# The tails' product of the second layer moved ahead of the seven products, with the first sum of weights brought behind it

## The chip, the cores and the metric

The kernel runs on one core of one Trainium2 chip. The metric is device time in microseconds for one execution of the whole program, all eight batches. The engines' names are those of the profile: PE is TensorE (matmuls; PEld its weight loads), DVE is VectorE, ACT is ScalarE, POOL is GpSimd, and SP is SyncE, which here issues the DMAs (its queue is shown as SPq).

## The reference

The inputs q, k and v have 8 batches, 8 heads, 576 tokens and 64 dimensions a head, in float32. Attention keeps for each query the 32 largest scores:

```python
scores = scale * np.matmul(q, k.transpose(0, 1, 3, 2))
kth = np.partition(scores, -top_k, axis=-1)[..., -top_k:-top_k + 1]
scores = np.where(scores >= kth, scores, -1000000000.0)
# softmax over the last axis, then
attn_out = np.matmul(attn, v)
```

Its result, with the heads side by side, is x: 576 tokens of 512 numbers for each batch. Then follow a Fourier mix and a two-layer perceptron:

```python
X = np.fft.fft(np.fft.fft(x, axis=1), axis=2)
u = x + np.real(X)
un = (u - mean(u)) / np.sqrt(var(u) + 1e-06)      # over the 512 numbers of a token
out = u + np.maximum(un @ w_ch1, 0.0) @ w_ch2     # w_ch1: 512 x 2048, w_ch2: 2048 x 512
```

The change concerns only the last product, `hidden @ w_ch2`.

## The kernel before

**Two streams of work.** The attention of a batch has 36 steps (4 pairs of heads, nine items of query rows a pair). A loop over steps, numbered i, writes for each of them the instructions of all engines in the order in which the engines take them. The order is fixed by hand; only the data decide when an instruction starts. VectorE spends its time on the selection of the 32 largest (lines 425 and 427). TensorE computes scores (371, 386, 401), transposes q, k and the attention's result (308, 604) and multiplies probabilities by v (564).

The perceptron of batch b runs beside the attention of batch b+1. `mlp_units(b)` makes a list of units, each a small closure with a cost in microseconds, and the loop puts into each step as many of them as fit beside its attention work (`some`, a room worked out from costs). The first unit on the list always goes first. A unit whose data are late holds TensorE, since TensorE takes its instructions in the order written.

**Tiling of the perceptron.** A batch's 576 tokens are five tiles: four of 128 and one of 64, the tails (tile 4, 32 tokens of each half). Chunk 0 is tiles 0, 1 and 4, chunk 1 is tiles 2 and 3. For each chunk come 16 units `hidden` (line 957; matmuls 966, then ACT's 970 writes hT), and then the second layer, in one of two ways:

- Plain (`back`, line 986): one tile against all of w2, which lies in SBUF. For the tails these are four units of eight matmuls, at line 1032. `tails_done` (1041) follows the fourth: ACT copies half of the result (1048); one step later (`late_next`) VectorE adds it (1052) and adds to x (1054), and SP stores two blocks of 32 tokens (1059).
- By seven products (`fast`, line 1068): two token tiles as a 2 x 2 block matrix against w2 as a 2 x 2 block matrix, with seven block products in place of eight. The products use sums of hT's blocks (`mix`, on POOL, line 1108) and sums of w2's blocks. Each product is two units of eight matmuls at line 1163, with results in the PSUM tiles cv, cw and, in the last batch, cz.

Batch 0 uses plain products only. Batches 1 to 6 use seven products for tiles 0 and 1 of chunk 0, and plain ones for the tails and for chunk 1. The last batch, 7, uses seven products in both chunks.

**Where the sums of weights lie.** T1, T2, T3 and T4 (four sums) and copies of the plain blocks B12 and B21 lie in DRAM (`w2_parts`), 1 MB each. They have no place of their own in SBUF: `bring(o, place, part)` (line 906, the DMA at 909, on SP) writes half of one, 512 KB, over the part of w2 that is not needed at the time. `w2_12` and `w2_21` are the two places, the off-diagonal blocks of w2. In the order of the products in batches 1 to 6:

- `begin` brings T1 to `w2_12`. It stands on the list behind the first unit `hidden` of its chunk.
- p2 reads the plain `w2_21`, and each half then brings T4 there. p1 reads a diagonal block, which is never written over.
- p5 reads T1, and each half then brings T2. p4 reads T4, and brings T3.
- p6 reads T2, and brings B12, so that `w2_12` is plain again. p3 reads a diagonal block.
- p7 reads T3, and brings B21: now `w2_21` is plain again.

A plain product needs all of w2 plain, and so both B12 and B21. In the kernel before the tails follow p7. In the last batch T3 and T4 have another place (`w_s`), `begin` brings T1 and T4, and B21 isn't brought.

**SP's queue.** SP issues one DMA after another in the order written. Beside the sums of weights these are, at each step: planes of the attention's probabilities to DRAM (485, 488), the turn that reads them back transposed (506), loads of q, k and v (240 to 288) and stores of results (1059, 1142). A DMA whose source or place isn't ready holds those behind it.

**Sums on POOL.** `later` (929) puts an addition on a list that each step takes from as time allows; `need` makes it, and those ahead of it, be written at once. The key `("x", 4)` is POOL's addition of p6's result to x, which uses the same tile (`ct`) that the tails' copies use.

## Time and profile before

| what | value |
|---|---|
| median of three runs | 1872.15 us (1869.95 to 1873.57) |
| the profiled execution, its own time | 1871.9 us |
| its span in the profile | 1870.1 us |
| mean granted TensorE clock | 0.957 |
| busy: PE / DVE / ACT / POOL | 1702.5 / 1580.6 / 1292.9 / 913.2 us |
| tails, line 1032: 256 matmuls | 75.0 us busy, 22.6 us idle before them |
| seven products, cw at line 1163: 448 matmuls | 102.8 us busy |
| 512 KB sums of weights, 82 DMAs to w | median 4.7 us from issue to landing |

Busy time is the sum of the durations of an engine's instructions, and it may hold instructions that run longer at a lower clock. "Idle before" is the time in which an engine stood still ahead of an instruction, put down to what it waited for last. The share over the whole span is a mean over stages. The first 260 us hold attention alone; the last 200 us are the perceptron of the last batch with little or no attention beside it; in between attention and perceptron run side by side. The granted clock is the share of TensorE's full speed that the profile records. A step of the loop is some 5.7 us long there (36 steps a batch, about 205 us from one batch to the next).

### The profile page before, as it was taken

To read this page: it belongs to the slowest core of one execution; us is meant where nothing else is said; L and a number is where in the kernel's file an instruction comes from. 1 tells how busy PE (TensorE), PEld (TensorE's weight loads), DVE (VectorE), ACT (ScalarE), POOL (GpSimd) and SP (SyncE) were. 2 spreads that over 40 slices of the span, in tenths; PEclk is the share of its full clock that TensorE was granted. 3 is DMA by queue.
4 is the path that set the end of the run, shared out by engine and by line. 5 is a ranking of instruction groups with operands and counts; after the bars stand their busy time and mean duration, and the time that the engine had idled before them with its cause. 6 is when DMAs were issued, how large, how long until landed. Compare 5 with 4: busy or idle time off the path is not lost.

```text
span 1870.1 us, 26944 instructions
## 1 busy us (share of the span) xinstructions
PE 1702.5 (91%) x8134; PEld 1086.0 (58%) x8134; DVE 1580.6 (85%) x3301; ACT 1292.9 (69%) x3104; POOL 913.2 (49%) x1278
## 2 busy tenths in 40 slices
PE   5667699789899998999999999999999899999999
PEld 3344364355456654565566565666567555677677
DVE  7999989789899999998999899998999899863110
ACT  6878658568687778776788678867788678652100
POOL 4768643444745366354654466355545365250012
PEclk8878899899899999999999999999999999999999
DMA  5333025661467755686476755684476655530132
GB/s 168 104 98 109 20 59 157 165 168 32 121 157 191 193 134 135 154 203 152 106 176 151 211 127 133 165 223 123 120 174 173 178 126 146 133 105 1 56 104 79
DMA packets 516576, 249.16 MB, mean 133 GB/s; under 512 B 398288, under 2 KB 506448, under 8 KB 516432
## 3 DMA queue, kind: packets, MB, share of 16 engines
q1 hardware_dynamic: 515664, 247.23, 50.9%
q8 instruction: 65, 1.06, 0.2%
q14 instruction: 79, 0.65, 0.1%
q10 hardware_dynamic: 768, 0.21, 0.0%
HBM read 93.63 MB, written 84.74 MB: 95 GB/s over the span
## 4 chain that ended last, share of the span: by engine, by line
PE 50%; DVE 22%; POOL 9%; ACT 7%; issue 7%; DMA 3%; SPq 2%; POOLq 0%; DVEq 0%; ACTq 0%
PE hp L966 19%; DVE m L425 10%; DVE wk L427 10%; PE o L564 5%; PE cp L993 4%; POOL wk L451 4%; PE sp L401 4%; PE cp L1032 3%; PE cv L1163 3%; PE cw L1163 3%; ACT wk L448 2%; POOL fg L651 2%; PE yp L755 2%; DMA w<-w_parts 1%; PE sp_t L371 1%
## 5 line engine op out<-in xcount | busy, mean ns | idle before, releaser
L451 POOL TENSOR_TENSOR wk<-S,wk 128x576 f32<-128x576 f32 x288 | 409.6, 1422 | 505.8 <-ACT wk L448 504.6
L425 DVE MAX8 m<-wk 128x8 f32<-128x576 f32 x864 | 626.5, 749 | 6.0
L966 PE MATMUL hp<-unT,w 128*128 128x256 f32 (+1 forms) x2048 | 526.0, 409 | 4.7 <-ACT hT L970 4.0
L966 PEld LDWEIGHTS hp<-unT,w 128*128 128x128 f32 x2048 | 380.3, 191 | 111.1 <-issue 12.0
L427 DVE MATCH_REPLACE8 wk<-m,wk 128x576 f32<-128x576 f32 x576 | 427.6, 742 | 0.0
L472 ACT COPY wk<-S 128x576 uint16<-128x576 uint16 x468 | 289.8, 671 | 0.0
L448 ACT ACTIVATE wk<-S,nt 128x576 f32<-128x576 f32 x288 | 223.7, 777 | 87.0 <-POOL nt L434 85.7
L993 PE MATMUL cp<-w,hT 128*128 128x512 f32 x512 | 234.0, 598 | 0.0
L425 DVE MAX8 m<-S 128x8 f32<-128x576 f32 x288 | 213.8, 742 | 18.7 <-ACT S L375 18.7
L459 ACT ACTIVATE S<-wk,nt 128x576 f32<-128x576 f32 x234 | 184.2, 787 | 51.7 <-POOL wk L451 49.9
L427 DVE MATCH_REPLACE8 wk<-m,S 128x576 f32<-128x576 f32 x288 | 213.7, 742 | 0.0
L564 PE MATMUL o<-PT,v 128*64 128x256 f32 (+3 forms) x1440 | 198.4, 421 | 11.5 <-ACT x L627 6.9
L970 ACT ACTIVATE hT<-hp 128x320 f32<-128x320 f32 (+1 forms) x256 | 103.5, 413 | 141.7 <-PE hp L966 139.9
L401 PE MATMUL sp<-kT,qT 64*128 64x512 f32 (+1 forms) x528 | 172.5, 675 | 12.9 <-ACT means L1351 5.7
L564 PEld LDWEIGHTS o<-PT,v 128*64 128x64 f32 x1440 | 114.4, 155 | 87.6 <-issue 18.8
L404 ACT COPY S<-sp 128x512 f32<-128x512 f32 (+1 forms) x264 | 141.9, 587 | 31.0 <-PE sp L401 30.1
L993 PEld LDWEIGHTS cp<-w,hT 128*128 128x128 f32 x512 | 94.0, 193 | 90.3 <-issue 89.5
L1108 POOL TENSOR_TENSOR hT<-hT 128x512 f32<-128x512 f32 x64 | 81.3, 1273 | 115.6 <-ACT hT L970 97.1
L434 POOL TENSOR_TENSOR nt<-m,cc 128x2 f32<-128x2 f32 x288 | 58.1, 202 | 158.3 <-DVE m L425 157.4
L371 PEld LDWEIGHTS sp_t<-kt,qT 128*128 128x128 f32 x320 | 51.1, 195 | 112.1 <-issue 63.3
L1163 PE MATMUL cw<-w,hT 128*128 128x256 f32 x448 | 102.8, 380 | 1.7 <-POOL hT L1108 1.4
L1032 PE MATMUL cp<-w,hT 128*64 128x512 f32 x256 | 75.0, 659 | 22.6 <-DMA w<-w_parts 22.6
(160 smaller groups left out, 2156.6 us busy)
## 6 DMA issues: line engine op xcount, KB each, us to landing
planes<-wk SPq DMA_DIRECT2D x208, 288.0 KB, 2.7
w<-w_parts SPq DMA_DIRECT2D x82, 512.0 KB, 4.7
space<-in_moe_w_ch_dram SPq DMA_DIRECT2D x32, 512.0 KB, 3.7
nat<-in_q_dram SPq DMA_DIRECT2D x128, 64.0 KB, 2.4
v<-in_v_dram SPq DMA_DIRECT2D x64, 128.0 KB, 3.0
out_dram<-x SPq DMA_DIRECT2D x32, 256.0 KB, 2.6
nat<-in_k_dram SPq DMA_DIRECT2D x62, 128.0 KB, 3.0
planes<-wk SPq DMA_DIRECT2D x52, 144.0 KB, 2.7
```

The source lines that it names most:

```text
L401: nc.tensor.matmul(sp[r], lhsT=qT[hd, q_cols], rhs=kT[hd, :], start=True, stop=True)
L404: nc.scalar.copy(out=s_t[r, keys], in_=sp[r])
L425: ops.append(lambda src=src, m8=m8: nc.vector.max(out=m8, in_=src))
L427: ops.append(lambda src=src, m8=m8: nc.vector.match_replace(w, m8, src, NEG))
L448: nc.scalar.activation(out=w, in_=Ssb[i], func=AF.Relu, scale=-FAR, bias=Nt[i][:, 1:2])
L451: nc.gpsimd.tensor_tensor(out=w, in0=Ssb[i], in1=w, op=ALU.subtract)
L459: nc.scalar.activation(out=Ssb[i] if by_dma(i) else w, in_=w, func=AF.Exp, bias=Nt.pop(i)[:, 0:1], accum_out=den_t[pair % 3][:, c:c + 1],)
L472: nc.scalar.copy(out=words[:, half, :], in_=src[:, half, :])
L564: nc.tensor.matmul(o[D * e:D * (e + 1), c0:c1], lhsT=vv[:, c, e, :], rhs=pt[:, NF if c == NF else (NF + 1) * e + c, c0:c1], start=(c == 0) ...
L966: nc.tensor.matmul(hp[:, 0:w], lhsT=w1[:, dt, P * it:P * (it + 1)], rhs=unT[:, dt, 0:w], start=(dt == 0), stop=(dt == NDT - 1),)
L993: nc.tensor.matmul(cp, lhsT=hT[:, it, P * n:P * (n + 1)], rhs=w2[:, it, :], start=(it == 0), stop=(it == NIT - 1),)
L1163: nc.tensor.matmul(dst, lhsT=h()[a][:, kc, :], rhs=rhs_of(kc), start=start and kc == 0, stop=kc == NK - 1, skip_group_check=True,)
```

## The change

In batches 1 to 7, in chunk 0:

- The four units of the tails' plain product go ahead of the seven products, behind the 16 hidden units and the first POOL sum (`mix "21"`). At that time w2 is still plain.
- `begin`, with T1's two DMAs (in the last batch also T4's), is no longer a unit behind the first `hidden`. It is called at the end of the tails' fourth unit, behind `tails_done`. It can't go sooner, because T1 is written over a block that the tails read.
- `need((b, 0, "x", 4))` in `tails_done` is gone, since that addition now comes later than the tails.

The order of p2, p1, p5, p4, p6, p3 and p7 stays, as do the DMAs that each of them issues. Chunk 1 of the last batch, which has no tails, keeps its `begin` behind its first hidden unit. Batch 0 and the plain products of chunk 1 are not touched. Each engine has the same number of instructions.

For batch 3 the steps of the loop in which the units stand are as follows: before, p2 in 174 to p7 in 179 and the tails in 180 and 181; after, the tails in 174 and 175, p2 and half of p1 in 176, the rest of p1 and half of p5 in 177, the rest of p5 and p4 in 178, p6 in 179, p3 in 180 and p7 in 181. Chunk 1's first hidden unit is in step 182 in both.

```diff
-        cps, cts, stored = {}, [], []
+        cps, cts, stored, begins = {}, [], [], []
...
             if part == 3:
                 tails_done(cp, free)
+                if begins:
+                    begins.pop()()
 
         def tails_done(cp, free):
 
-            if b and not last:
-                need((b, 0, "x", 4))
             ct, rs = ct_of(4), rs_of[b]
...
-            return (0.0, begin, "hidden"), [
+            return begin, [
                 (0.0, lambda: mix("21", "21", "22", ALU.add), "back")
             ] + [
                 (1.75, lambda f=f, part=part: f(part), "back")
...
             if seven:
                 begin, products = fast(ch)
-                units.insert(1 - NIT, begin)
-                units += products
+                if ch == 0:
+                    begins.append(begin)
+                else:
+                    units.insert(1 - NIT, (0.0, begin, "hidden"))
+                mix_first = products.pop(0)
+                units.append(mix_first)
             for t in [t for t in CHUNKS[ch] if t == 4 or not seven]:
                 units += [
                     (1.75, lambda ch=ch, t=t, p=p: back(ch, t, p), "back")
                     for p in range(4 if t == 4 else 8)
                 ]
+            if seven:
+                units += products
```

## The prediction

> **What bounds the kernel now.** I read the busy shares first, then windows of about one batch, then TensorE's waits, then the rows around the one wait that the change aims at, and last the queue that issues the transfers. The page:

> ```profile
> PE 1702.5 (91%) x8134; PEld 1086.0 (58%) x8134; DVE 1580.6 (85%) x3301; ACT 1292.9 (69%) x3104; POOL 913.2 (49%) x1278
> L1032 PE MATMUL cp<-w,hT 128*64 128x512 f32 x256 | 75.0, 659 | 22.6 <-DMA w<-w_parts 22.6
> w<-w_parts SPq DMA_DIRECT2D x82, 512.0 KB, 4.7
> ```

> TensorE is busiest, but the mean hides two regimes. Busy time per stretch (columns: stretch, length, PE, PEld, DVE, ACT, POOL, granted clock, DMA share, GB/s):

> ```profile
> 640.00:845.00 205.00, 188.38 (x918) 120.32 (x916) 202.29 (x420) 159.44 (x382) 107.98 (x159) 0.99 0.62 158
> 1050.00:1255.00 205.00, 199.01 (x964) 125.96 (x964) 191.76 (x399) 157.49 (x375) 105.20 (x155) 0.98 0.62 159
> 1024.00:1054.00 30.00, 25.51 (x107) 17.30 (x106) 29.63 (x63) 17.20 (x38) 16.67 (x19) 0.92 1.01 274
> ```

> Up to 845 us VectorE is full (202.3 of 205) and TensorE's waits cost little. From 845 to 1665 each batch takes 205 us, TensorE is busy 199 of them and VectorE 191.8: a wait of TensorE is paid there. The third line is the stretch of seven products in batch 3: the DMA engines are full (1.01), which matters for landings below. In a whole period (1050 to 1255) TensorE's one wait above half a microsecond is the tails' product (line 1032) for a sum of weights:

> ```profile
> 1041.12 3.62 PE L1163 MATMUL cw<-w,hT 128*128 128x256 f32 x16
> 1044.66 1.07 PE L1032 MATMUL cp<-w,hT 128*64 128x512 f32 x2
> 1050.23 3.67 PE L1032 MATMUL cp<-w,hT 128*64 128x512 f32 x6 [4.49 <-DMA w<-w_parts]
> 1053.83 1.33 PE L308 MATMUL tpq<-ident,nat 128*128 128x128 f32 x5
> 1055.09 2.42 PE L1032 MATMUL cp<-w,hT 128*64 128x512 f32 x8
> 1060.72 1.94 PE L1032 MATMUL cp<-w,hT 128*64 128x512 f32 x8
> ```

> After 4.49 us of idling the same work also runs slower: six matmuls take 3.67 us where eight take 1.94 once warm. The granted clock by microsecond says why:

> ```profile
> 1048.00:1049.00 1.00, 0.00 (x0) 0.00 (x0) 0.97 (x3) 0.00 (x0) 0.00 (x0) 1.00 1.08 351
> 1050.00:1051.00 1.00, 0.77 (x2) 0.29 (x4) 1.00 (x2) 0.00 (x0) 0.00 (x0) 0.50 1.08 344
> 1055.00:1056.00 1.00, 1.00 (x4) 0.30 (x4) 1.00 (x2) 1.00 (x3) 0.00 (x0) 0.50 0.02 7
> 1057.00:1058.00 1.00, 1.00 (x10) 0.45 (x8) 1.00 (x2) 1.00 (x3) 0.81 (x1) 1.00 0.52 116
> ```

> SP's queue, where every sum of weights is issued (line 909), between turns (line 506) and planes (lines 485, 488) of the attention:

> ```profile
> 1033.19 2.64 SPq L506 DMA_TRANSPOSE PT<-planes  x1
> 1035.94 1.23 SPq L488 DMA_DIRECT2D planes<-wk  x2
> ...
> 1039.09 1.92 SPq L506 DMA_TRANSPOSE PT<-planes  x1
> 1041.11 0.58 SPq L485 DMA_DIRECT2D planes<-wk  x1
> ...
> 1045.87 1.16 SPq L909 DMA_DIRECT2D w<-w_parts  x2
> ```

> The last pair, B21, can start only when p7 has read its place (1044.7) and lands 4.3 us later: that is the wait.

> **What the change removes.** Plain w2 is no longer needed behind p7, but in front of p2, where it has lain since the batch before. So the wait at line 1032 goes, in batches 1 to 6. Its waits by batch are 1.61, 6.22, 4.49, 4.59, 5.37 and 0.30 us (sum 22.6, as on the page). The full price of one event, in batch 3: from the first tails matmul (1044.66) to the next hidden unit (1066.26) is 21.60 us. Warm, the same work is 4 parts of 1.75 (the last batch's 7.09 for 32) plus 5.7 of transposes, attention and scores between (start to start 0.55, 2.79, 0.59, 0.42, 1.05, 0.33), so 12.73. The event costs 8.9: 4.5 of wait and 4.4 of half clock. In batch 5 the cold part is shorter (eight matmuls at 2.03 instead of 2.42), so I put 4.0 beside each wait of batches 2 to 5: 10.2, 8.5, 8.6, 9.4, together 36.7 us. Batch 1 lies where VectorE is full, and its 1.61 and batch 6's 0.30 left the clock up: about 0.5 together.

> What is late next is VectorE: around the event it waits 3.7 (line 591), 2.5 (line 1052) and 1.0 us (line 608), all results of a late TensorE; 7.2 us per batch, and its other waits of the period are 3.3. A gain above some 7.2 per batch (four batches: 29) would find VectorE full.

> **What it adds: T1 on the path.** T1 leaves from a roomy place (behind the first hidden unit) for one after the tails' last part. Count from t0, the end of the tails, which is where p2 started before. TensorE then has p2 and p1 (four parts of 1.73 to 1.9), a batch of transposes and 1.4 of scores: p5, T1's reader, is due at t0+9.1. T1 goes first on SP: two issues of 0.55, landing 4.7 (median; 3.7 to 8.1): t0+6. Slack 3; cost 0, and at the slowest landing still 0. T4 follows p2's parts at t0+4 and +5 behind one plane, lands by +10, and p4 wants it at +12.6. Cost 0, cover 2.6.

> **What it adds: T2 between p5 and p6.** Before, T2's pair and half of T3 went out in a row (one entry of three at 1026.8) and p6 came after p4 with 1.4 of scores between. Now p5 crosses a step's edge, and in SP's program the queue behind T4 is: six natural loads of q (3.0 us, as at 1030.13 and 1032.21), two stores of the tails (line 1059, now in this place, moved ahead of two turns), turn, two planes, T2's first half, turn, plane, T2's second half. A DMA also waits here for the landing of the one eight places ahead on SP (the turn at 1033.19 began when T2's second half had landed, 1033.2), so the stores wait for T4's landing, t0+10.4. Turn 2.65: +13.05. Planes 1.23: +14.3, T2's first half, landing 4.4 to 5.4 (this batch's landings while the engines were full): +18.75 to +19.75. Its reader, p6's first part, is due at +17.4: wait 1.35 to 2.35. The turn behind waits for its planes to land (1.92) and one plane goes: +18.95, second half lands +23.35 to +24.35. p6's second part is due at +19.1: in all 4.25 to 5.25 of waiting, which I take as 4.75, split about 1.85 and 2.9. Whether the clock falls is open: 2.91 us of idling dropped it elsewhere in this trace, 2.23 at 394.8 did not. Bounds: 0 (it stays up) and 4.0 (as after line 1032); the two halves are broken by a product of 1.73, which is nearer to the small case, so 2.25. The new event costs 7.0 (4.25 to 9.25), in each of batches 2 to 5, total 28; in batch 1 0 to 1, VectorE being full.

> [...]

> **Everything else.** T3, B12 and B21 follow as before, each with more than a product of cover: p7, T3's reader, is three products behind p4; B12 and B21 are not wanted before the next batch's tails or the second chunk, 16 hidden units (over 35 us) later. The mix "21" stays ahead; its halves (POOL, 1.25 each) now have the tails as cover, a gain nobody waits for. The dropped need of the POOL addition "x4" removes nothing: order on that tile is kept by the data. The number of instructions on each engine is the same. The tails' copies on ACT (line 1048) and additions on VectorE come six steps earlier: 1.2 and 1.4 us of work that merely moves, hidden on ACT (157 busy of 205) and paid by nobody on VectorE, which waits 7.2 us at the old place and has its own queue full of selection work at the new one.

> **Last batch.** There begin stood behind the first hidden unit, with 16 units of cover; the tails followed p7 without waiting (32 matmuls in 7.09). Now T1 and T4 are issued after the tails' stores, which SP holds until VectorE is done: in this trace 2.8 us from the tails' end (1814.19) to the stores (1817.01), then 0.9 and four transfers, landing 5.0 to 5.6. T1's halves land at t0+7.6 to +8.8 with p5 due at +7.0: a loss of 0.6 to 2.5, taken as 1.5. This stretch has no other work to hide it.

> **Sum.** Batches 2 to 5: 36.7 - 28 = 8.7 gained; batches 1 and 6: 0.5 gained; last batch 1.5 lost: 7.7. The profiled execution took 1871.9 us (span 1870.1, 1.8 around it), 0.25 below the median 1872.15. 1872.15 - 7.7 = 1864.5.

> **Rivals.**
> (a) The clock holds at p6, or T2 lands two microseconds sooner, because fewer DMAs are in flight than in the stretch before. Without the clock an event costs 4.25 to 5.25, which gives 4 x 4.0 to 4.9, less 1.0 for the other batches; with the landing sooner too it costs 2.75, 4 x 6.4 less 1.0: 1847 to 1857. VectorE's 7.2 per batch ends it at 1844. For it: six weight transfers in the first 20 us as before, none more. Against: SP's order above.
> (b) Slower or equal by p6. The wait goes from the tails to p6 and grows there: T2's second half stands behind two turns, the DMA engines are full, and its landing is 6 us or more instead of 4.9. It decides when wait plus half clock exceeds 9.2 per batch, that is at a landing at t0+24.3 with the full 4.0 of clock, or +26 with 2.25. With landings at +26 and full clock the event is 10.9: 4 x 1.7 + 1.0 lost, 1880. Against: landings of 4.4 to 5.8 in this very stretch.
> (c) T1 is late at p5 as well: only if it lands over 8 us after its issue, three above the median. 1870 to 1878.
> (d) VectorE or the attention becomes the bound: the tails' stores and T1 put the turns back by 3 us, and attention units wait for them; gain 2 or less, 1870.

> **How the numbers follow.** Chances: forecast (1858 to 1869) 0.46, (a) 0.16, (b) 0.23, (c) 0.06, (d) 0.09. A change under 0.2% (3.7 us) can't be told from none with these runs. Faster (below 1868.4): 0.44 of the forecast's 0.46 and (a), 0.60. Same: the rest of the forecast's, (d), half of (c), a third of (b), some 0.21. Slower: 0.19. Range: from 1850 (most of (a) inside) to 1878 (most of (b) inside). Where the forecast's own case holds, 1858 to 1869.

> **What would show it.** Right: line 1032 without waits; a wait of the product's line (1163) at p6 of 4 to 5 us per batch, in two pieces, for a weight transfer; VectorE's 3.7 and 2.5 smaller; the last batch longer by 1 to 2. Wrong if: p5 waits for T1, p6's waits are above 6 or below 2, the granted clock stays at 1.00 behind them (then (a)), or half clock lasts 6 us behind them (then (b)), or the period stays at 205 with VectorE full.

## The result, and the profile after

The changed kernel takes 1863.03 us (median of 11 runs, 1857.08 to 1868.84) against 1872.15 us (11 runs, 1869.83 to 1877.33). The ratio is 0.9953, with a 95% interval of [0.9937, 0.9968]: 8.8 us faster, between 6.0 and 11.8. The forecast was 1864.5 with a range of 1850 to 1878.

The profiled execution happens to be the slowest of the eleven (1868.84 us, span 1867.0), so its profile shows only 3 us of the gain. What it shows of places is sound; what it shows of sizes has to be read beside the runs below. First the page of the changed kernel: TensorE's busy time is what it was (1702.5 before), and the idle time of 22.6 us at line 1032 is gone. In its place cw at line 1163, idle for 1.7 us before, stands 20.3 us idle. The first line is cw's before the change, the other two are from the page after.

```profile
L1163 PE MATMUL cw<-w,hT 128*128 128x256 f32 x448 | 102.8, 380 | 1.7 <-POOL hT L1108 1.4
PE 1702.6 (91%) x8134; PEld 1092.4 (59%) x8134; DVE 1583.8 (85%) x3301; ACT 1293.7 (69%) x3104; POOL 913.9 (49%) x1278
L1163 PE MATMUL cw<-w,hT 128*128 128x256 f32 x448 | 110.8, 398 | 20.3 <-DMA w<-w_parts 14.9
```

TensorE's timeline shows where: at p6, in two pieces per batch. These are the rows of batch 3 (1044 and 1049) and of batch 5 (1449 and 1454), with p3 behind them; all four pieces end with a weight transfer.

```profile
1044.01 1.97 PE L1163 MATMUL cw<-w,hT 128*128 128x256 f32 x8 [1.48 <-DMA w<-w_parts]
1048.65 1.97 PE L1163 MATMUL cw<-w,hT 128*128 128x256 f32 x8 [2.68 <-DMA w<-w_parts]
1050.45 1.89 PE L1163 MATMUL cv<-w,hT 128*128 128x256 f32 x8
...
1448.87 1.96 PE L1163 MATMUL cw<-w,hT 128*128 128x256 f32 x8 [1.68 <-DMA w<-w_parts]
1454.47 3.75 PE L1163 MATMUL cw<-w,hT 128*128 128x256 f32 x8 [3.64 <-DMA w<-w_parts]
1458.01 3.07 PE L1163 MATMUL cv<-w,hT 128*128 128x256 f32 x8
```

The forecast's queue on SP can be laid beside the real one. The tails of batch 3 end at 1024.8, which is t0.

```profile
1028.70 1.17 SPq L909 DMA_DIRECT2D w<-w_parts  x2
1029.92 2.04 SPq L240 DMA_DIRECT2D nat<-in_q_dram  x4
1032.00 0.94 SPq L279 DMA_DIRECT2D nat<-in_q_dram  x2
1033.38 1.85 SPq L1059 DMA_DIRECT2D out_dram<-x  x2
1035.27 2.43 SPq L506 DMA_TRANSPOSE PT<-planes  x1
1037.82 1.22 SPq L488 DMA_DIRECT2D planes<-wk  x2
1039.13 0.55 SPq L909 DMA_DIRECT2D w<-w_parts  x1
1040.99 1.90 SPq L506 DMA_TRANSPOSE PT<-planes  x1
1042.99 0.58 SPq L485 DMA_DIRECT2D planes<-wk  x1
1043.67 1.84 SPq L909 DMA_DIRECT2D w<-w_parts  x3
```

T2's first half leaves at t0+14.3 (forecast 14.3), the second at t0+18.9 (18.95). The two waits are 1.48 and 2.68 us (1.35 to 2.35, and some 2.9).

How much a batch gains hangs on the clock behind p6's waits. The windows by microsecond show it at 1.00 in batch 3, and at 0.50 from 1454 to 1460 in batch 5, whose eight matmuls take 3.75 instead of 1.97 us.

```profile
1048.00:1049.00 1.00, 0.35 (x2) 0.35 (x3) 1.00 (x3) 0.00 (x0) 0.00 (x0) 1.00 1.07 373
...
1453.00:1454.00 1.00, 0.00 (x0) 0.00 (x0) 1.00 (x4) 0.00 (x0) 0.00 (x0) 0.78 1.04 347
1457.00:1458.00 1.00, 1.00 (x3) 0.75 (x3) 1.00 (x3) 0.00 (x0) 0.00 (x0) 0.50 1.10 308
1461.00:1462.00 1.00, 1.00 (x9) 0.95 (x8) 0.97 (x3) 0.45 (x1) 1.00 (x2) 1.00 1.15 243
```

A useful yardstick for all that follows is the length of a batch. I take it from the first plain matmul of chunk 1 (line 993) in one batch to that in the next, on TensorE's timeline of each profiled execution. The last column runs from batch 6 to the end of the last product.

| kernel | b0-b1 | b1-b2 | b2-b3 | b3-b4 | b4-b5 | b5-b6 | b6-end |
|---|---|---|---|---|---|---|---|
| before | 241.8 | 218.1 | 204.7 | 204.8 | 205.2 | 190.5 | 164.0 |
| changed | 243.6 | 215.6 | 200.7 | 203.9 | 204.9 | 189.7 | 165.9 |
| changed, no T2 (e1) | 241.8 | 212.5 | 196.9 | 197.3 | 198.6 | 189.8 | 165.6 |
| before, no B21 (e8) | 242.9 | 208.2 | 196.4 | 196.3 | 196.6 | 189.2 | 163.5 |
| e7 | 244.9 | 211.4 | 197.8 | 198.3 | 198.4 | 189.7 | 163.5 |

The column b2-b3 holds batch 3's products, b3-b4 those of batch 4, and so on. In the profiled execution the clock stayed up in one of batches 2 to 5, batch 3, which takes 200.7 us. It fell in the other three: batches 4 and 5 take 203.9 and 204.9, nearly as long as before, and batch 2 takes 215.6 instead of 218.1. The last batch is 1.9 us longer.

### The profile page after: what moved, and what is told of

Its sections match the earlier page's. It is cut to its first block, busy times and chain, and to the rows that moved or that the text cites. A ratio compares the mean times of both kernels' runs of the same rounds, so it can differ in the third digit from the quotient of the medians.

```text
span 1867.0 us, 26996 instructions
## 1 busy us (share of the span) xinstructions
PE 1702.6 (91%) x8134; PEld 1092.4 (59%) x8134; DVE 1583.8 (85%) x3301; ACT 1293.7 (69%) x3104; POOL 913.9 (49%) x1278
## 3 DMA queue, kind: packets, MB, share of 16 engines
q8 instruction: 65, 1.06, 0.3%
## 4 chain that ended last, share of the span: by engine, by line
PE 57%; DVE 12%; POOL 10%; ACT 10%; issue 6%; DMA 4%; SPq 1%; POOLq 0%; DVEq 0%; ACTq 0%
PE hp L966 21%; PE o L564 6%; DVE m L425 5%; DVE wk L427 5%; PE cp L993 5%; PE cw L1163 4%; PE sp L401 4%; POOL wk L451 4%; PE cv L1163 4%; PE cp L1032 3%; ACT wk L448 2%; PE yp L755 2%; POOL fg L651 2%; DMA w<-w_parts 2%; PE sp_t L371 2%
## 5 line engine op out<-in xcount | busy, mean ns | idle before, releaser
L966 PEld LDWEIGHTS hp<-unT,w 128*128 128x128 f32 x2048 | 380.0, 191 | 110.4 <-issue 10.2
L1163 PE MATMUL cw<-w,hT 128*128 128x256 f32 x448 | 110.8, 398 | 20.3 <-DMA w<-w_parts 14.9
L1163 PEld LDWEIGHTS cw<-w,hT 128*128 128x128 f32 x448 | 86.2, 198 | 37.0 <-issue 16.8
## 6 DMA issues: line engine op xcount, KB each, us to landing
w<-w_parts SPq DMA_DIRECT2D x82, 512.0 KB, 4.7
space<-in_moe_w_ch_dram SPq DMA_DIRECT2D x32, 512.0 KB, 3.7
```

The source lines that it names most:

```text
L966: nc.tensor.matmul(hp[:, 0:w], lhsT=w1[:, dt, P * it:P * (it + 1)], rhs=unT[:, dt, 0:w], start=(dt == 0), stop=(dt == NDT - 1),)
L1163: nc.tensor.matmul(dst, lhsT=h()[a][:, kc, :], rhs=rhs_of(kc), start=start and kc == 0, stop=kc == NK - 1, skip_group_check=True,)
```

## The experiments

All ratios are to the kernel before, run on the same chip beside them; "us below" is (1 - ratio) x 1873. By this measure the changed kernel stands 8.8 below.

### The price of the new wait: no T2 (e1)

```diff
-                bring(T2, w2_12, part)
+                if last:
+                    bring(T2, w2_12, part)
```

> The changed kernel without T2's transfers in batches 1 to 6: p6 reads what lies there, so its results are not the reference's; everything else is left. Theory (the new wait at p6 is paid): its two waits, 4.2 to 5.3 us per batch in batches 2 to 5, and the half clock behind them (in two or three of the four batches, some 3 us each) go, and six 1 MB transfers with them. VectorE still has 6 to 8 us of idling per batch, so most of it shows: 17 to 28 us below the changed kernel's 1863, that is 1835 to 1846. Rival (VectorE or the attention is the bound by now, p6's wait hides behind it): within 4 us of 1863, with VectorE's waits gone in exchange.

Measured: 1845.88 us (1845.26 to 1852.26), ratio 0.9864 [0.984, 0.9889], 25.5 below, so 16.7 below the changed kernel. The wait is paid, as the theory has it, but its price lies just under the 17 to 28 that were expected. Why is in TensorE's waits of this kernel around the products of batches 3 to 5 (895 to 1510 us; columns: us in total, times, longest):

```profile
PE o L564 <- DMA PT<-planes: 4.3, 3, 2.4
```

With p6's wait out of the way the attention's product (line 564) waits for a turn: 0.76, 1.12 and 2.38 us in batches 3 to 5, and 2.83 in batch 2, at the same place. The kernel before has no such wait in these batches. This is a cost of the new order that was not in the forecast; e11 and e12 come back to it.

### The tails' stores later (e2)

```diff
+                if last or not b:
+                    store()
+                else:
+                    at(now[0] + 4, "load2", store)
```

> The changed kernel with the tails' two stores (line 1059) put four steps later in batches 1 to 6, nothing else moved. Theory (the order on SP holds T2): in batch 3 the stores stood at 1033.38 to 1035.23 and waited for T4's landing; without them the turn starts at about 1033.4 instead of 1035.27, T2's halves are issued 1.9 us sooner, and p6's waits fall from 4.2 to 5.3 us per batch to 2.3 to 3.4, with the clock up in most. 8 to 15 us below 1863: 1848 to 1855. Rival (the DMA engines are full, the landing depends on the bytes ahead and not on the order): T2 is issued sooner and lands later after its issue, p6's waits stay above 4, 1860 to 1866.

Measured: 1859.68 us (1856.5 to 1862.38), ratio 0.993 [0.9908, 0.9952], 13.1 below, 4.3 better than the changed kernel. In batch 3 T2's halves now leave at 12.5 and 17.2 us behind the tails' end, 1.9 and 1.8 sooner, as the theory says. The order on SP does hold T2. But p6's first wait went and the second stayed, in one piece, and the clock fell behind it in all four batches: eight matmuls take 2.95 to 3.65 us, where the changed kernel has 1.97 at full clock (line 1163 is 1169 in this kernel):

```profile
842.21 2.97 PE L1169 MATMUL cw<-w,hT 128*128 128x256 f32 x8 [3.11 <-DMA w<-w_parts]
1043.58 2.95 PE L1169 MATMUL cw<-w,hT 128*128 128x256 f32 x8 [2.86 <-DMA w<-w_parts]
1245.68 3.65 PE L1169 MATMUL cw<-w,hT 128*128 128x256 f32 x8 [3.71 <-DMA w<-w_parts]
1446.80 3.39 PE L1169 MATMUL cw<-w,hT 128*128 128x256 f32 x8 [3.05 <-DMA w<-w_parts]
```

Less waiting in all, but in one piece: the expected 8 to 15 us became 4.

### p3 ahead of p6 (e3)

```diff
-                for f in (p2, p1, p5, p4, p6, p3, p7) for part in range(2)
+                for f in ((p2, p1, p5, p4, p6, p3, p7) if last else (p2, p1, p5, p4, p3, p6, p7))
+                for part in range(2)
```

> The changed kernel with p3 ahead of p6 in batches 1 to 6 (the store of the first token tile moves behind p6 with it). Theory (T2 lacks cover): p3's two parts, 3.5 us, run while T2 lands; p6's waits fall to 0 to 1.5 us per batch, the clock stays up. 14 to 26 us below 1863: 1837 to 1849. Rival: p3's sums on POOL (mix 12, behind mix 11) or ACT's copy of p5's result, which lies in the same bank half, are now late, and the wait moves from p6 to p3: 1858 to 1866, with a wait of line 1163 for POOL or ACT above 2 us per batch.

Measured: 1869.36 us (1866.04 to 1874.61), ratio 0.9981 [0.9968, 0.9993], 3.6 below: worse than the change alone, and neither theory. p6's waits did fall, to 0.5 to 2.0 us per batch, and neither POOL nor ACT holds p3. A new wait of the attention's product took over, up to 4.9 us long. In this kernel's waits from 895 to 1510 us:

```profile
PE o L564 <- DMA PT<-planes: 11.9, 3, 4.9
PE cw L1163 <- DMA w<-w_parts: 4.0, 3, 2.0
```

### The last batch in the old order (e4)

```diff
-                if ch == 0:
+                if ch == 0 and not last:
                     begins.append(begin)
...
+                if last:
+                    units += products
...
-            if seven:
+            if seven and not last:
                 units += products
```

> The changed kernel with the last batch in the old order (begin behind the first hidden unit, tails behind p7), batches 1 to 6 as changed. Theory: the last batch loses 1.5 us by the change (0.63 and 0.91 us of waits at p5), and gets them back, as its p6 waited 0.2 before: 1861.5, 1.3 to 2.5 below the changed kernel, and its profile shows no wait at p5. Rival: the last batch loses nothing, 1863.

Measured: 1862.6 us (1859.58 to 1865.49), ratio 0.9943 [0.9924, 0.9961], 10.7 below. The interval holds the changed kernel's 0.9953, so the times alone do not settle 2 us. The profile does: the last stretch takes 163.5 us, where it takes 165.9 with the change, and no wait is left at p5. The changed kernel's rows there are these:

```profile
1792.19 1.97 PE L1163 MATMUL cv<-w,hT 128*128 128x256 f32 x8 [0.63 <-DVE x L1121]
1795.07 1.97 PE L1163 MATMUL cv<-w,hT 128*128 128x256 f32 x8 [0.91 <-DMA w<-w_parts]
```

### p5 in one step (e5), with the later stores (e6), and the old last batch too (e7)

```diff
-                (1.75, lambda f=f, part=part: f(part), "back")
-                for f in (p2, p1, p5, p4, p6, p3, p7) for part in range(2)
+                (1.75, lambda f=f, part=part: f(part), "back")
+                for f in (p2, p1) for part in range(2)
+            ] + ([...] if last else [
+                (1.75, lambda: (p5(0), p5(1)), "back"), (3.5, lambda: p4(0), "back"),
+            ]) + [(1.75, lambda: p4(1), "back")] + [
+                (1.75, lambda f=f, part=part: f(part), "back")
+                for f in (p6, p3, p7) for part in range(2)
```

> The changed kernel with p5's two parts as one unit in batches 1 to 6, so that both stand in one step, ahead of the next turn; T2's two halves then go out together. Theory (T2's second half is late because a turn and a plane of the next step stand before it on SP): the second half is issued about 4 us sooner, p6's second wait goes, its first (1.2 to 2.0) stays and takes in what is left; 1 to 2.5 us per batch in all, clock up. 8.8 us faster than before as the change is, and 10 to 16 more: 18 to 25 below before. Rival (the transfer itself is slow, the DMA engines being full, so that both halves land later): p6 still waits 3 to 4 us per batch, 9 to 12 below before.

> Both of the last two edits: p5's parts in one step, and the tails' stores four steps later, in batches 1 to 6. Theory: T2's halves go out at about p5's end (12.5 and 13.1 us behind the tails' end) and land before p6 wants them; p6's waits under 1 us per batch, clock up, VectorE full: 22 to 28 below before, about what the kernel without T2 gave (25.5). Rival: as for the last, and the stores four steps later collide with turns: 12 to 18 below before.

> The same with the last batch in the old order as well. 1.5 to 2.5 below the one before it: 24 to 30 below before, 1843 to 1849.

Measured: e5 1854.39 us (1852.78 to 1858.04), ratio 0.989 [0.9873, 0.9907], 20.6 below. e6 1850.73 us (1847.79 to 1852.42), ratio 0.9866 [0.985, 0.9882], 25.1 below. e7 1847.63 us (1844.38 to 1852.19), ratio 0.9856 [0.9836, 0.9876], 27.0 below. All three are where the theory puts them. In e5 T2's halves go out as one row on SP, and p6 waits 1.8 to 2.8 us per batch, in batches 2 to 4 in one piece. The clock did not stay up in all of them as expected: these are p6's 16 matmuls in batches 2, 3 and 4, at 5.38 us where it fell and 3.69 where it didn't.

```profile
842.38 5.38 PE L1163 MATMUL cw<-w,hT 128*128 128x256 f32 x16 [2.78 <-DMA w<-w_parts]
1042.67 3.69 PE L1163 MATMUL cw<-w,hT 128*128 128x256 f32 x16 [2.28 <-ACT S L375]
1241.70 5.38 PE L1163 MATMUL cw<-w,hT 128*128 128x256 f32 x16 [1.77 <-POOL wk L451]
```

In batches 2 to 5 of e6 p6's waits are 0.9 us or less, and e7 has none above 0.5 there. So what stood ahead of T2 on SP made the new wait, not the transfer's own speed: a turn and a plane ahead of its second half, and the tails' stores ahead of both. Nor do T2's bytes cost anything that these runs can tell: e6 keeps all its transfers and is 16.3 us below the changed kernel, where e1, without T2's, is 16.7 below. e7 computes the same as both kernels and is faster than either. What still waits in it, from 895 to 1510 us, is the attention:

```profile
PE o L564 <- DVE wk L427: 3.6, 2, 2.0
PE o L564 <- DMA PT<-planes: 1.6, 1, 1.6
```

### The price of the old wait: no B21 (e8)

```diff
-                if not last:
-                    bring(B21, second, part)
```

> The kernel before without B21's two transfers behind p7 in batches 1 to 6: the tails and chunk 1 then multiply by what T3 left there, so results are not the reference's. It prices the wait that the change removes, by itself. Theory: line 1032 has no wait, the clock stays up; four events of 8.5 to 10.2 us (36.7) are open, of which VectorE's 7.2 per batch lets through 29: 25 to 29 below before. Rival (the wait was partly cover for something else, as p6 or a turn): 10 to 20 below before, with a wait of TensorE for turns or weights in its place.

Measured: 1837.29 us (1834.36 to 1838.95), ratio 0.9794 [0.9778, 0.981], 38.6 below. This is more than expected: a batch takes 196.4 us instead of 204.8, so 8.4 came through where VectorE was to let 7.2 pass. In one such batch (columns as before) TensorE is busy for 195.18 of 196.40 us and VectorE for 191.44: now TensorE is the bound, with 1.2 us left to wait.

```profile
886.80:1083.20 196.40, 195.18 (x966) 124.99 (x965) 191.44 (x400) 157.63 (x377) 105.02 (x156) 1.00 0.65 160
```

The same run shows what the old event's work takes without the wait. In batch 3 the tails begin at 1034.43 and the next hidden unit at 1047.68, 13.25 us later; with the wait it was 21.60. The difference of 8.35 us is the batch's whole gain (204.7 to 196.4).

```profile
1034.43 1.94 PE L1032 MATMUL cp<-w,hT 128*64 128x512 f32 x8
1036.30 0.77 PE L308 MATMUL tpq<-ident,nat 128*128 128x128 f32 x5
1047.68 1.89 PE L966 MATMUL hp<-unT,w 128*128 128x256 f32 x8
```

### Useless work against the drop of the clock (e9, e10)

```diff
+                if part and 2 <= b <= 5:
+                    idle = bank([P, DM], f"idle_{b}")
+                    for _ in range(6):
+                        nc.tensor.matmul(
+                            idle[:, lo], lhsT=w1[:, 0, 0:P], rhs=w1[:, 0, lo], start=True, stop=True
+                        )
                 c = product("w", lo, "11", first, part, False)
```

That is e10, on the changed kernel, ahead of p6's second part. e9 has ten of these matmuls, on the kernel before, behind p7.

> The kernel before with ten extra matmuls (128x256, results unused, 4.3 us at full clock) between p7 and the tails in batches 2 to 5. The wait for B21 ends when it ended before; TensorE only stands still for less of it. It splits the old event into wait and clock. Theory (4.0 to 4.4 of each event's 8.9 are half clock, set off by the idling): useless work makes the kernel faster, 4 events x 3.5 to 4.4: 12 to 18 us below before, with line 1032's wait down to 0 to 2 us and the clock at 1.00 behind it. Rival (the clock drop is not due to the idling, or what it costs is hidden): within 4 us of before, or slower by up to 4.

> The changed kernel with six such matmuls (2.6 us) between p6's two parts in batches 2 to 5, where the second wait is 2.7 to 3.6 us. Theory (the new event is 4.2 us of wait, and 4 more in those batches where the idling drops the clock, which it does in some executions and not in others): the drops go and the waits stay; 4 to 8 us below the changed kernel, 13 to 17 below before (ratio 0.991 to 0.993), and the spread between executions, 12 us for the changed kernel, shrinks to that of before, 7. Rival: clock not the matter, the ratio stays at 0.995 and the spread too.

Measured: e9 1868.53 us (1866.53 to 1871.71), ratio 0.9967 [0.9955, 0.9978], 6.2 below; e10 1860.43 us (1857.51 to 1862.26), ratio 0.992 [0.9907, 0.9933], 15.0 below, 6.2 better than the changed kernel. Both signs are the theory's: 4.3 us of useless matmuls per batch make the old kernel faster. In batch 3 they cut the tails' wait from 4.49 to 0.96 us, and the granted clock is 1.00 in the microseconds from 1046, 1051 and 1053 on, where the kernel before stands at 0.50 from 1049.3 to 1056.1. e10 has the size expected, too; its five executions lie within 4.8 us, though five are too few to say that the spread is smaller than the changed kernel's 11.8. e9 has half the size expected. Its rows in batch 3 tell why:

```profile
1042.23 3.62 PE L1163 MATMUL cw<-w,hT 128*128 128x256 f32 x16
1045.69 4.48 PE L1229 MATMUL idle<-w 128*128 128x256 f32 x20
1050.23 1.07 PE L1032 MATMUL cp<-w,hT 128*64 128x512 f32 x2
1052.26 1.93 PE L1032 MATMUL cp<-w,hT 128*64 128x512 f32 x6 [0.96 <-DMA w<-w_parts]
```

Six tails matmuls take 1.93 us instead of 3.67. But from p7's end (1045.7) to the first hidden unit (1065.5) it is 19.8 us, of which 4.5 are filler and 1.0 a wait: 14.3 us are left, all at full clock, where the kernel before needs 21.6 - 4.5 = 17.1 beside its wait. So the half clock cost 2.8 us there. The other 1.06 us between 14.3 and e8's 13.25 is the stop itself: the first eight tails matmuls, which stop after two, take 2.93 us beside their wait (1050.23 to 1054.12, less 0.96), where e8's eight in a row take 1.87. The old event of 8.35 us is thus 4.49 of wait, 1.06 of stopping and starting, and 2.8 of clock. B21's reader also went on a microsecond later after p7's end than before (6.6 us against 5.6), which took part of the 2.8 back.

### Why p3 ahead of p6 brought nothing (e11, e12)

e11 is e3 with p5 in one step. e12 is e11 with this:

```diff
-                    bring(B12, w2_12, part)
+                    at(now[0] + 3, "load2", lambda: bring(B12, w2_12, part))
...
-                    bring(B21, second, part)
+                    at(now[0] + 2, "load2", lambda: bring(B21, second, part))
```

In the last batch this also puts B12 behind T1 of the second chunk, so p5 there multiplies by the plain block, and e12's results are not the reference's. The instructions are the same, and the stretch from batch 6 to the end takes as long as in e11 (165.9 and 165.8 us), so the gain does not come from there.

> p3 ahead of p6 together with p5's parts in one step. It asks why p3 ahead of p6 alone brought nothing: there p6's waits were 1.2 to 2.0 and the attention's product (line 564) then waited 3.0 to 4.9 us for a turn, with a drop of the clock. Theory A (p6's leftover wait, which stands directly ahead of the attention there, starts the chain that makes the turn late): without it p6 waits 0 and line 564 under 2; 20 to 26 below before. Theory B (the order itself does it: p6 later means B12 later, beside the planes of the next turn): line 564 still waits 3 to 5 us per batch, 3 to 8 below before.

> The last one (p3 ahead of p6, p5 in one step) with the transfers of B12 and B21 put three and two steps later, behind the turn that line 564 waited for. Theory (1 MB each of B12 and B21 beside that turn and its planes made them late: its planes landed 4.2 us after their issue with the DMA engines full): line 564's wait falls from 4.2 to 5.2 us per batch to under 2, the clock stays up; 18 to 27 below before. Rival (the turn is late for VectorE's selection, not for the DMA engines): line 564 still waits 3 us or more, and it stays at 5 to 10 below before.

Measured: e11 1867.07 us (1865.24 to 1868.08), ratio 0.9958 [0.9942, 0.9973], 7.9 below; e12 1844.76 us (1842.07 to 1852.49), ratio 0.9842 [0.9819, 0.9865], 29.6 below. In e11 p6 waits for nothing, and the attention's product still waits 4.2 to 5.2 us per batch: theory A falls. In e12 those waits are 0.7 to 1.0 in three of the four batches, 2.2 in the other. (e12's profiled execution is its slowest, 1852.49 us; in batch 1, outside these four, line 564 waits 5.8 us there.) From 895 to 1510 us, first e11:

```profile
PE o L564 <- DVE wk L427: 9.1, 2, 4.9
PE o L564 <- DMA PT<-planes: 4.6, 1, 4.6
```

and e12:

```profile
PE o L564 <- DVE m L425: 1.7, 2, 1.0
PE o L564 <- DMA PT<-planes: 1.0, 1, 1.0
```

(The releaser named changes with what came last; the place is the same.) On SP in e11, B12, two loads of k, the plane and B21 follow one another, and the turn behind them starts 4.2 us after the plane's issue has ended:

```profile
1053.55 1.17 SPq L909 DMA_DIRECT2D w<-w_parts  x2
1054.77 1.09 SPq L267 DMA_DIRECT2D nat<-in_k_dram  x2
1055.91 0.74 SPq L271 DMA_DIRECT2D nat<-in_k_dram  x1
1056.75 0.65 SPq L485 DMA_DIRECT2D planes<-wk  x1
1057.50 1.89 SPq L909 DMA_DIRECT2D w<-w_parts  x2
1061.65 3.60 SPq L506 DMA_TRANSPOSE PT<-planes  x1
```

So in this order 2 MB of sums beside that plane and that turn delay the attention. In e12 they follow later, and the turn starts 2.1 us after the plane. e12 moves both transfers, so it does not tell which of the two matters more.

## Why the prediction was right, point by point

**What bounds the kernel: right.** Line 1032's wait was on the path in batches 2 to 5 and went. The period of 205 us that the prediction gives from 845 to 1665 us holds only up to batch 5; the one to batch 6 is 190.5. Batch 1, where VectorE is full (busy 202.3 of 205 us from 640 to 845), and batch 6 gave nothing that can be read.

**The old event, 36.7 us and 0.5: right, one of its parts not.** e8 prices it at 38.6 (35.6 to 41.6), and the rows of e8's batch 3 at 8.35 us where the prediction had 8.9. The wait term (20.7) stands. The other term, 4.4 us in batch 3, was put down to half clock alone; it is 2.8 of clock, 1.06 of stopping and starting, and 0.5 by which the warm work was counted too short (12.73 for 13.25).

**VectorE as the cap, 7.2 per batch: too low.** Batches of e8 gained 8.3 to 9.9. VectorE's waits fall there from 10.5 us per batch (the prediction's 7.2 and 3.3) to 2.3, so 8.2 us of them hung on the late TensorE; of the 3.3 counted as fixed, 1.0 did too.

**T1 and T4 at no cost: right** in batches 1 to 6. Neither p5 nor p4 waits for a transfer.

**T2 at p6, 4.75 us per batch: right.** The waits sum to 4.78, 4.16, 4.41 and 5.32 us in batches 2 to 5, mean 4.67, in the place stated; e2 and e5 show the cause. (The profile puts the first pieces of batches 2 and 4 down to ACT and POOL, which came last there.) The clock's 2.25, a middle value between 0 and 4, is near too, but as a mean only: the clock fell in three of four batches of the profiled execution, for 6.8 us each, and e10 gets back 1.6 per batch (6.2 / 4). By the prediction's own list, half clock of 6 us behind p6 would have meant rival (b); it came in three batches, and (b)'s loss did not.

**The new event's sum of 28: mis-sized.** e1 prices it at 16.7. Behind p6's wait another one lies hidden, the attention's product waiting for its turn (0.8 to 2.8 us in e1, e6 and e7), so that taking p6's wait away gains less than its length. In e1 it sums to 7.1 us in batches 2 to 5, and there e1's four batches are together 7.8 us longer than e8's. The prediction looked at that turn only in rival (d), as put back by stores and T1. In e7's queue it is B21 that now stands right ahead of the turn (at 1054.99, the turn at 1057.22); before, no sum of weights did (the turn at 1060.91). That B12 and B21 delay it is shown by e12 for the order with p3 ahead of p6 only; for the changed kernel's own order it is argued from the queue, and no run moves them there.

So that 8.8 was measured where 7.7 was forecast is in part luck: the new wait was priced some 11 too high, and this crowding, in which e1 and e8 differ by some 13 (of which 2 in the last batch, and part of it may be B21's own absence from e8), was priced at nothing. The two nearly cancel.

**The last batch, 1.5: right.** Two waits of 0.63 and 0.91 us at p5; the stretch is 1.9 longer. The profile puts the first of the two down to VectorE; in e1, e2, e3, e5 and e6, whose last batch is the same, both end with the transfer, as the prediction had it.

**The rivals.** (b), the wait that moves to p6 and grows, has the right place but not the size; for single batches with a drop of the clock (204.9 against 205.2) it is nearly the case. (a) is what e5 to e7 made of it: 1847.6 to 1854.4.

## What to carry to other kernels

When a wait for a transfer is removed by reordering, follow each remaining transfer through its issuing queue in the new order: the forecast of p6's wait came out to 0.6 us in each batch because each entry ahead of T2 was counted. Then ask what the moved transfers now lie beside; with p3 ahead of p6 the last two met the attention's own DMAs, and only moving these too let the gain through. And where TensorE's idling may drop its clock, a wait's price is its length, plus some 1 us for the stop itself (1.06, from e8's and e9's rows of one batch), plus some microseconds more in the batches where the clock falls (2.8 in that batch): a forecast needs all three terms, and one profiled execution does not tell the last.

## What the runs showed of the hardware

Whether a gap of some 2 us drops the clock does not hang on its length alone. Behind p6's gaps of 2.80 us and more it fell each time (2.86, 3.05, 3.11 and 3.71 in e2, 2.80, 3.22 and 3.64 in the changed kernel). Below that it fell behind 1.77 and 2.78 us in e5, and not behind 2.28 there, nor behind 2.68 in the changed kernel.

```profile
1047.42:1050.83 3.41, 2.18 (x10) 1.97 (x11) 3.38 (x9) 0.17 (x1) 0.00 (x0) 1.00 1.10 348
1450.19:1453.61 3.42, 0.64 (x3) 0.21 (x2) 3.39 (x8) 0.00 (x0) 0.79 (x1) 0.99 1.00 269
...
1041.15:1044.57 3.42, 1.90 (x9) 1.72 (x10) 3.35 (x8) 2.26 (x7) 3.42 (x4) 1.00 1.21 277
1239.14:1242.55 3.41, 1.64 (x8) 1.10 (x7) 3.41 (x8) 3.41 (x8) 3.41 (x3) 1.00 1.20 305
```

The clock fell behind the second and the fourth, where TensorE was busy for 19% and 48% of the stretch, and not behind the others (64% and 56%). Ahead of each of the ten drops from 600 to 1690 us in the traces of the kernel before and the changed one it was busy for 31% or less of the last 3.41 us (0 to 6% before, 20 to 31% in the changed kernel). What else the drop hangs on is not shown: for whoever forecasts it, the one behind a gap of some 2 us remains a chance.

In e5 a gap of 1.77 us already cost 16 matmuls 1.7 us (5.38 against 3.69). Whether such chances make the changed kernel's executions lie further apart (11.8 us, against 7.5 before) is not shown. Work whose result nobody reads made both kernels faster, each by 6.2 us (e9, e10).

A 512 KB sum of weights took 4.7 us from issue to landing in the median of the run, and 4.2 to 6.8 (median 5.0) in the changed kernel's batch 3 between 1020 and 1052 us, where the DMA engines were 91% busy. e12 gained 21.7 us on e11 by issuing B12's and B21's transfers three and two steps later.
